# One load of two heads, or two loads of one head each: splitting the key and value loads of a decode attention kernel

## The chip, the cores and the metric

The kernel runs on one core of one Trainium2 chip. The metric is the time of one execution on the device, in microseconds (us), as the median of several runs. The profile is of one further execution. TensorE is called PE here, VectorE DVE, ScalarE ACT, GpSimd POOL; SP is the engine that does nothing here but issue transfers. All large transfers come from SP's queue and are carried out by the core's 16 DMA engines.

## The reference

One decode step for two sequences: a layer norm, attention of 32 query heads over the last 4096 positions of 8 cached key and value heads, and a small gated branch whose result multiplies the attention's output.

```python
xn = _layernorm(x)                                    # x: [2, 1, 512]
# attention: Hq, Hkv, Sk, Dh = 32, 8, 32768, 128; W = 4096; rep = 4
q = (xn @ wq).reshape(B, Sq, Hq, Dh).transpose(0, 2, 1, 3)
k = jnp.repeat(k_cache[:, :, Sk - W:, :], rep, axis=1)
v = jnp.repeat(v_cache[:, :, Sk - W:, :], rep, axis=1)
p = _softmax(jnp.einsum("bhqd,bhkd->bhqk", q, k) * Dh ** -0.5)
s = jnp.einsum("bhqk,bhkd->bhqd", p, v) ... @ wo      # wo: [4096, 512]
# gated branch: gelu, layer norm over half of it, two small products
g = _silu(_B_ref(xn, w_in, w_sp, b_sp, w_out))
return x + s * g
```

Everything is float32. Of each head 4096 rows of 512 bytes are read, 2 MiB, for the keys and again for the values. With 2 sequences and 8 heads that is 64 MiB of keys and values; the four weight matrices add 21.25 MiB.

## The kernel before, in words

**Units.** The 16 pairs of sequence and head are taken two heads at a time: 8 units (`NU`), each with a load of keys (`k`) and a load of values (`v`) of 4 MiB. A load fills one slot, a tile of 128 partitions with 32 KB each (`SLOT` = 8192 elements, 64 rows of the cache). Even partitions hold the unit's first head, odd ones its second: partition 2i has rows 64i to 64i+63 of the first head, partition 2i+1 the same rows of the second. The two heads lie 16 MiB apart in the cache, so the source of a load is written by hand as 64 steps of 32 KB, times 2 heads, times 8192 elements.

**The ring.** All large loads share four slots (pool `ring`). In the order in which SP issues them: `win`, `wout`, two halves of `wq`, then keys and values in the order k0, k1, v0, k2, v1, k3, v2, and so on to k7, v6, v7, and at last the output weights `wo` in pieces of 2, 2, 2, 1, 0.5, 0.25 and 0.25 MiB. A load waits until the slot's earlier content is used up: for keys, the last of four transposes on DVE (`turn`, tile `kt`), for values, the last of 16 products on PE (`values`, tile `acc`). After each load of keys or values but the first, SP also issues a small transfer from x into `rows`, of 2, 3, ... 15 and last 1 rows of 128 bytes (`load_rows`). No engine reads `rows`.

**Counters.** A transfer tells that it has landed by a counter (semaphore). Eight of them (`DMAHW0` to `DMAHW7`) are handed to the transfers in turn, in the order of the program. A transfer is issued only when the transfer that had the same counter before it, eight transfers back, has landed.

**A unit's work.** DVE turns the keys by four transposes (`kt<-k`), PE multiplies them with the queries (`sh`), ACT copies the result (`shs`), PE adds the shares into the unit's scores (`s`), DVE and ACT make the softmax of the unit before (`m`, `mg`, `mx`, `nb`, `p`, `pT`), and PE multiplies with the values (`acc`). The order on every engine is the order in which the program is written. The last unit is followed by the product with `wo` (`part`, `so`), the multiplication with the gate (`res`), and the store.

Names in the rows below carry a buffer's number, which differs between the two programs: keys of unit 3 are `k_296` before and `k_301` after, values of unit 3 `v_305` before and `v_313` after.

Of the kernel before, what the change touches and what calls it, by code (L numbers as in the profile page):

```python
# [14 lines left out]
P = 128  # L15
HQ, DH = 32, 128
# [26 lines left out]
def kernel(  # L43
# [14 lines left out]
    pe, dve, act, sp = (InOrder(tc, e) for e in (nc.tensor, nc.vector, nc.scalar, nc.sync))  # L58
    B, _, D = x.shape
    _, HKV, SK, _ = k_cache.shape  # L60
    W = min(4096, max(256, SK // 4))
# [8 lines left out]
    J = 2 * W // P  # L70
    JC = 512 // 32
    NCH = J // JC
    SLOT = J * DH
# [7 lines left out]
    def slot(name):  # L81
        return ring.tile([P, SLOT], F32, tag="slot", name=name)
# [18 lines left out]
    for a in range(2):  # L101
        t = slot(f"wq{a}")
# [11 lines left out]
    def load_unit(cache, u, name):  # L114

        b, w = divmod(u, NU // B)
        t = slot(f"{name}{u}")
        first = cache[b, 2 * w, SK - W :, :]
        src = bass.AP(tensor=first.tensor, offset=first.offset, ap=[[SLOT, P // 2], [SK * DH, 2], [1, SLOT]])
        sp.dma_start(t, src)  # L120
        return t.rearrange("p (j d) -> p j d", d=DH)


# [297 lines left out]
    for n in range(NU + 1):  # L421
        if n < NU:
            units[n].k = load_unit(k_cache, n, "k")
            if n > 0:
                load_rows(2 * n)
        if n > 0:
            units[n - 1].v = load_unit(v_cache, n - 1, "v")
            if n < NU:
                load_rows(2 * n + 1)
            else:  # L430
                load_rows(1)
# [4 lines left out]
    j = 0  # L436
    for i, piece in enumerate(pieces):
        t = slot(f"wo{i}").rearrange("p (j d) -> p j d", d=D)
        at = 0
        for n in piece:  # L440
            sp.dma_start(t[:, at : at + n, :], wo_v[:, j : j + n, :])
            blocks += [(t, at + a) for a in range(n)]
            at, j = at + n, j + n
# [49 lines left out]
    for n in range(EARLY):  # L493
        t, a = blocks[n]
# [5 lines left out]
    for n in range(EARLY, 32):  # L500
        if n == LATE:
            spread_quarters(so, parts, start=False, stop=False)
        t, a = blocks[n]
# [37 lines left out]
```

## Time and profile before

| | |
|---|---|
| time, median of 3 runs | 218.21 us (217.74 to 218.59) |
| span of the profiled execution, first to last instruction | 216.4 us |
| busy, PE / DVE / ACT | 154.9 / 108.6 / 44.0 us |
| moved by DMA | 89.55 MB, mean 414 GB/s over the span |
| chain that ended last, by engine | DMA 62%, DVE 19%, PE 16% |
| loads of keys, and of values | 8 and 8, 4096 KB each |

The profiled execution's own time is its span of 216.4 us and what lies around it; the median of the runs is 1.8 us longer than that span. The chain that ended last is found by going back from the last instruction to what released it, and so on. Times in the timeline count from the span's start.

### The profile page before, as it was taken

Reading aid. Unit: us, or ns where it says so; the run is one execution under the profiler, and the core shown is the slowest. Engines: PE = TensorE matmul, PEld = TensorE weight load, DVE = VectorE, ACT = ScalarE, POOL = GpSimd, SP = SyncE. Lnnn points to the kernel's source line nnn. Section 1 sums busy time; section 2 is a strip of 40 time slices with the busy share of each in tenths; the row PEclk is TensorE's granted clock in tenths of the full one; section 3 lists DMA queues with packets and bytes.
Section 4 is the critical chain, followed back from the end, with each engine's and each line's share of the span. In section 5 each row is a group of like instructions: output and inputs, shape, how many; then the busy total and the mean of one; then the engine's idle time right before and its main releaser. Section 6 shows DMA issues by size and latency. Waiting matters only on the chain.

```text
span 216.4 us, 2244 instructions
## 1 busy us (share of the span) xinstructions
PE 154.9 (72%) x866; PEld 43.0 (20%) x866; DVE 108.6 (50%) x176; ACT 44.0 (20%) x109; POOL 2.6 (1%) x14
## 2 busy tenths in 40 slices
PE   0173176518959957994995699459959967997973
PEld 0121121101212211221221222222222212231311
DVE  3505312569778089238806941695479089331001
ACT  5003310002221331042121304120331241242001
POOL 4000000000000000000000000000000000000000
PEclk9998569955997995899799589956996997999698
DMA  7999999999999999999999999999999999999990
GB/s 255 424 436 442 430 432 427 442 430 424 448 418 448 409 448 418 436 424 436 426 433 430 424 442 421 442 424 436 424 430 430 415 454 418 448 394 430 412 365 23
DMA packets 4169, 89.55 MB, mean 414 GB/s; under 512 B 686, under 2 KB 702, under 8 KB 1088
## 3 DMA queue, kind: packets, MB, share of 16 engines
q1 hardware_dynamic: 4152, 89.42, 96.8%
q8 instruction: 7, 0.11, 0.2%
q14 instruction: 2, 0.02, 0.0%
q10 hardware_dynamic: 8, 0.00, 0.0%
HBM read 89.41 MB, written 0.00 MB: 413 GB/s over the span
## 4 chain that ended last, share of the span: by engine, by line
DMA 62%; DVE 19%; PE 16%; issue 1%; DVEq 0%; SPq 0%
DMA k<-in_A_k_cache_dram 49%; DVE kt L37 16%; DMA wo<-in_A_wo_dram 8%; DMA win<-in_B_w_in_dram 5%; PE sh L37 5%; PE s L37 4%; PE z L37 3%; PE acc L37 2%; PE mo L37 1%; DVE pT L37 1%; PE so L37 1%; DVE m L37 1%; PE oT L37 0%; DVE mg L37 0%; DVE mx L37 0%
## 5 line engine op out<-in xcount | busy, mean ns | idle before, releaser
L37 DVE STREAM_TRANSPOSE kt<-k 128x2048 f32<-128x2048 f32 x32 | 72.7, 2295 | 41.6 <-DMA k<-in_A_k_cache_dram 41.6
L37 PE MATMUL sh<-kt,qbd 128*32 128x512 f32 x256 | 41.0, 704 | 17.8 <-DVE kt L37 17.7
L37 ACT ACTIVATE shs<-sh 128x512 f32<-128x512 f32 x32 | 19.1, 597 | 119.1 <-PE sh L37 119.1
L37 PE MATMUL s<-shs,add_dq 128*128 128x512 f32 x64 | 40.5, 739 | 0.0
L37 PE MATMUL acc<-v,pT 128*32 128x512 f32 x256 | 33.0, 657 | 0.2 <-DVE pT L37 0.2
L37 PEld LDWEIGHTS s<-shs,add_dq 128*128 128x128 f32 x64 | 11.0, 215 | 29.7 <-issue 25.4
L37 PEld LDWEIGHTS sh<-kt,qbd 128*32 128x32 f32 x256 | 6.5, 115 | 38.4 <-issue 23.9
L37 PEld LDWEIGHTS acc<-v,pT 128*32 128x32 f32 x256 | 7.8, 121 | 26.6 <-issue 19.0
L37 PE MATMUL mo<-l,same_r 128*128 128x2 f32 x16 | 3.5, 287 | 10.6 <-ACT p L37 10.6
L37 ACT ACTIVATE o<-acc,wd 128x128 f32<-128x128 f32 x32 | 9.1, 372 | 3.4 <-PE acc L37 3.4
L37 PE MATMUL part<-wo,oT 128*32 128x512 f32 x56 | 8.2, 720 | 1.8 <-DMA wo<-in_A_wo_dram 1.5
L37 ACT ACTIVATE p<-s,nb 128x256 f32<-128x256 f32 x16 | 7.6, 488 | 7.2 <-DVE nb L37 6.9
L37 PE MATMUL z<-win,xnT 128*32 128x448 f32 x32 | 5.6, 873 | 4.8 <-DMA win<-in_B_w_in_dram 4.8
L37 PE MATMUL q_ps<-wq,xnT 128*32 128x512 f32 x64 | 7.3, 594 | 1.9 <-DMA wq<-in_A_wq_dram 1.9
L37 PE MATMUL col<-o,sel 128*32 128x512 f32 x16 | 8.3, 601 | 0.4 <-ACT o L37 0.4
L37 DVE TENSOR_REDUCE m<-s 128x2 f32<-128x512 f32 x8 | 5.4, 670 | 5.4 <-PE s L37 5.4
L37 PE MATMUL y<-wout,hT 128*32 128x512 f32 x14 | 3.4, 1020 | 3.8 <-issue 3.8
L37 DVE TENSOR_TENSOR res<-so,gate 128x128 f32<-128x128 f32 x1 | 0.3, 290 | 11.7 <-PE so L37 11.7
L37 DVE STREAM_TRANSPOSE pT<-p 128x512 f32<-128x512 f32 x8 | 5.4, 674 | 1.2 <-ACT p L37 1.2
L37 ACT ACT_TABLE_LOAD x4 | 5.1, 1283 | 1.9 <-issue 1.9
L37 PE MATMUL xnT_ps<-ident,xn 2*128 2x2 f32 x4 | 0.6, 252 | 6.7 <-DVE xn L37 6.7
L37 PEld LDWEIGHTS mo<-l,same_r 128*128 128x128 f32 x16 | 2.8, 218 | 12.2 <-ACT p L37 12.2
(106 smaller groups left out, 63.1 us busy)
## 6 DMA issues: line engine op xcount, KB each, us to landing
k<-in_A_k_cache_dram SPq DMA_DIRECT2D x8, 4096.0 KB, 26.8
v<-in_A_v_cache_dram SPq DMA_DIRECT2D x8, 4096.0 KB, 25.2
wq<-in_A_wq_dram SPq DMA_DIRECT2D x2, 4096.0 KB
wo<-in_A_wo_dram SPq DMA_DIRECT2D x3, 2048.0 KB
win<-in_B_w_in_dram SPq DMA_DIRECT2D x1, 3584.0 KB
wout<-in_B_w_out_dram SPq DMA_DIRECT2D x1, 1792.0 KB, 15.1
wo<-in_A_wo_dram SPq DMA_DIRECT2D x1, 1024.0 KB
wo<-in_A_wo_dram SPq DMA_DIRECT2D x1, 512.0 KB
```

The lines of the kernel that those rows point to most:

```text
L37: return self.tc.keep_in_program_order(call(*args, **kwargs))
```

## The change

Each load of 4 MiB becomes two loads of 2 MiB, one per head. The first writes the even partitions of the slot, the second the odd ones, both from 64 steps of 32 KB that lie one behind the other in the cache. The bytes, their places in the slot, and everything that reads them stay as they are.

```diff
         b, w = divmod(u, NU // B)
         t = slot(f"{name}{u}")
-        first = cache[b, 2 * w, SK - W :, :]
-        src = bass.AP(tensor=first.tensor, offset=first.offset, ap=[[SLOT, P // 2], [SK * DH, 2], [1, SLOT]])
-        sp.dma_start(t, src)
+        for a in range(2):
+            sp.dma_start(t[a::2, :], cache[b, 2 * w + a, SK - W :, :].rearrange("(i j) d -> i (j d)", j=J))
         return t.rearrange("p (j d) -> p j d", d=DH)
```

SP's instructions, before, from the keys of unit 3 (`k_296`) to the values of unit 3 (`v_305`), with the counters and engines that each waits for:

```order
L37 DMA k_296<-in_A_k_cache_dram 128x1x8192 [waits DMAHW0_49,DVE_49]
L37 DMA rows<-in_A_x_dram 6x32 [waits DMAHW1_49]
L37 DMA v_299<-in_A_v_cache_dram 128x1x8192 [waits DMAHW2_49,PE_49]
L37 DMA rows<-in_A_x_dram 7x32 [waits DMAHW3_49]
L37 DMA k_302<-in_A_k_cache_dram 128x1x8192 [waits DMAHW4_49,DVE_49]
L37 DMA rows<-in_A_x_dram 8x32 [waits DMAHW5_49]
L37 DMA v_305<-in_A_v_cache_dram 128x1x8192 [waits DMAHW6_49,PE_49]
```

Eight transfers are four loads here, so the counter that a load waits for belongs to the load whose slot it fills. The same stretch after (`k_301` to `v_313`):

```order
L37 DMA k_301<-in_A_k_cache_dram 64x8192 [waits DMAHW5_49,DVE_49]
L37 DMA k_301<-in_A_k_cache_dram 64x8192 [waits DMAHW6_49]
L37 DMA rows<-in_A_x_dram 6x32 [waits DMAHW7_49]
L37 DMA v_305<-in_A_v_cache_dram 64x8192 [waits DMAHW0_49,PE_49]
L37 DMA v_305<-in_A_v_cache_dram 64x8192 [waits DMAHW1_49]
L37 DMA rows<-in_A_x_dram 7x32 [waits DMAHW2_49]
L37 DMA k_309<-in_A_k_cache_dram 64x8192 [waits DMAHW3_49,DVE_49]
L37 DMA k_309<-in_A_k_cache_dram 64x8192 [waits DMAHW4_49]
L37 DMA rows<-in_A_x_dram 8x32 [waits DMAHW5_49]
L37 DMA v_313<-in_A_v_cache_dram 64x8192 [waits DMAHW6_49,PE_49]
L37 DMA v_313<-in_A_v_cache_dram 64x8192 [waits DMAHW7_49]
L37 DMA rows<-in_A_x_dram 9x32 [waits DMAHW0_49]
```

A load and its `rows` are three transfers now, so eight transfers back is the load three before (its second half, for a first half) or the load two before (its first half, for `rows`). The values of unit 3 wait for `DMAHW6`, which the second half of the keys of unit 3 had.

On DVE, the first transpose of unit 3's keys (`kt_0_556`) and its neighbours before:

```order
L37 STREAM_TRANSPOSE kt_2_529<-k_290 128x2048
L37 STREAM_TRANSPOSE kt_3_539<-k_290 128x2048
L37 STREAM_TRANSPOSE kt_0_556<-k_296 128x2048 [waits DMAHW0_49,PE_49]
L37 TENSOR_REDUCE m_2_565<-s_503 128x2 [waits PE_49]
L37 TENSOR_TENSOR mg_567<-m_2_565,spot 128x32 [waits DVE_49]
```

The same place after (`kt_0_572`):

```order
L37 STREAM_TRANSPOSE kt_2_545<-k_293 128x2048
L37 STREAM_TRANSPOSE kt_3_555<-k_293 128x2048
L37 STREAM_TRANSPOSE kt_0_572<-k_301 128x2048 [waits DMAHW6_49,DMAHW5_49,PE_49]
L37 TENSOR_REDUCE m_2_581<-s_519 128x2 [waits PE_49]
L37 TENSOR_TENSOR mg_583<-m_2_581,spot 128x32 [waits DVE_49]
```

The order is the same; the transpose waits for two counters, one of each half. At the end of SP's program, from the values of unit 7 (`v_326`) to `wo`'s smaller pieces, before:

```order
L37 DMA v_326<-in_A_v_cache_dram 128x1x8192 [waits DMAHW4_49,DVE_49]
L37 DMA rows<-in_A_x_dram 1x32 [waits DMAHW5_49]
L37 DMA wo_329<-in_A_wo_dram 128x4096 [waits DMAHW6_49,PE_49]
L37 DMA wo_329<-in_A_wo_dram 128x4096 [waits DMAHW7_49]
L37 DMA x_91<-in_A_x_dram 8x1x128 [waits DMAHW0_49,Pool_49]
L37 DMA wo_333<-in_A_wo_dram 128x4096 [waits DMAHW1_49,DVE_49]
L37 DMA wo_335<-in_A_wo_dram 128x2048 [waits DMAHW2_49,PE_49]
```

And after (`v_341` is unit 7's values):

```order
L37 DMA v_341<-in_A_v_cache_dram 64x8192 [waits DMAHW3_49,DVE_49]
L37 DMA v_341<-in_A_v_cache_dram 64x8192 [waits DMAHW4_49]
L37 DMA rows<-in_A_x_dram 1x32 [waits DMAHW5_49]
L37 DMA wo_345<-in_A_wo_dram 128x4096 [waits DMAHW6_49,PE_49]
L37 DMA wo_345<-in_A_wo_dram 128x4096 [waits DMAHW7_49]
L37 DMA x_91<-in_A_x_dram 8x1x128 [waits DMAHW0_49,Pool_49]
L37 DMA wo_349<-in_A_wo_dram 128x4096 [waits DMAHW1_49,DVE_49]
L37 DMA wo_351<-in_A_wo_dram 128x2048 [waits DMAHW2_49,PE_49]
```

The counters of `wo`'s pieces are the same by number, but they were last held by other transfers: the first piece now waits for the keys of unit 7 (second half) to have landed, `x` for the first half of unit 6's values, and the third piece for the second half of these.

## The prediction

> **What bounds the kernel now.** I read the page first: its slices and the shares of the chain that ended last.
>
> ```profile
> DMA  7999999999999999999999999999999999999990
> ...
> DMA 62%; DVE 19%; PE 16%; issue 1%; DVEq 0%; SPq 0%
> ```
>
> The DMA engines are busy in every slice from the second to the last but one, and the chain hangs on them most. Then I asked for the stretches between landings of keys (engine columns, granted clock, DMA share, GB/s):
>
> ```profile
> 20.00:95.50 75.50, 52.59 (x286) 13.90 (x286) 41.10 (x66) 14.96 (x34) 0.00 (x0) 0.80 1.00 432
> 95.50:134.40 38.90, 31.19 (x159) 8.12 (x158) 22.50 (x26) 9.30 (x26) 0.00 (x0) 0.87 1.00 430
> 134.40:173.30 38.90, 31.24 (x162) 8.91 (x161) 23.39 (x28) 7.95 (x21) 0.00 (x0) 0.82 1.00 431
> 173.30:211.30 38.00, 31.69 (x186) 8.73 (x185) 14.72 (x24) 7.70 (x25) 0.00 (x0) 0.91 0.97 413
> ```
>
> The DMA share is 1.00 from 20 to 173 us, at 430 to 432 GB/s, while DVE is busy for little more than half of each stretch (41.10 of 75.50, 22.50 of 38.90). Next the chain in order of time; its DMA pieces run from a load's issue to its landing (start, length):
>
> ```profile
> 0.73 11.25 DMA win<-in_B_w_in_dram
> ...
> 17.76 29.17 DMA k<-in_A_k_cache_dram
> ...
> 69.78 25.73 DMA k<-in_A_k_cache_dram
> ...
> 107.61 26.79 DMA k<-in_A_k_cache_dram
> ...
> 149.18 24.15 DMA k<-in_A_k_cache_dram
> ...
> 193.27 17.98 DMA wo<-in_A_wo_dram
> 211.25 0.04 issue
> ```
>
> By their place in SP's order these are k0, k3, k5 and k7: loads 1, 6, 10 and 14 of the sixteen. They land at 17.76 + 29.17 = 46.93, at 95.51, at 134.40 and at 173.33. Thirteen loads lie between first and last: 126.40 / 13 = 9.72 us each, and the three parts agree (9.72, 9.72, 9.73). Four MiB in 9.72 us are 431 GB/s. So the loads land on a grid of 9.72 us: load n at 46.93 + 9.72 (n - 1). The grid gives 192.8 for the last load (v7); 7.5 MiB of `wo`, down to its 0.5 MiB piece, add 18.2 us at that rate, 211.0, and the last landing on the chain is at 211.25. 216.4 - 211.25 = 5.1 us of tail follow. The kernel is one row of transfers with hardly a gap, plus a tail. A microsecond added to the row is a microsecond at the end; a microsecond saved elsewhere is nothing.
>
> Last, the waits: what SP waits for (total, times, longest),
>
> ```profile
> SPq L37 <- DVE kt L37: 97.6, 8, 14.7
> ```
>
> and what DVE waits for with its first transpose of each unit's keys:
>
> ```profile
> DVE kt L37 <- DMA k<-in_A_k_cache_dram: 41.6, 8, 7.5
> ```
>
> DVE waits for keys in every unit, so the consumers are early, and SP stands idle for 97.6 us until DVE frees a slot.
>
> **The change, part by part.**
>
> *The issues.* Sixteen loads become 32, so SP issues 16 more. The timeline of SP's queue has the price:
>
> ```profile
> 88.17 0.54 SPq L37 DMA_DIRECT2D k<-in_A_k_cache_dram  x1
> 88.76 0.48 SPq L37 DMA_DIRECT2D rows<-in_A_x_dram  x1
> 91.32 0.54 SPq L37 DMA_DIRECT2D v<-in_A_v_cache_dram  x1
> ...
> 107.61 0.54 SPq L37 DMA_DIRECT2D k<-in_A_k_cache_dram  x1
> ...
> 169.64 0.84 SPq L37 DMA_DIRECT2D wo<-in_A_wo_dram  x2
> 173.40 0.64 SPq L37 DMA_DIRECT2D x<-in_A_x_dram  x1
> 185.44 9.20 SPq L37 DMA_DIRECT2D wo<-in_A_wo_dram  x5
> ```
>
> 16 x 0.54 = 8.6 us of SP, beside the row of transfers. The cover is what is still queued when a load is issued: k5 goes out at 107.61, when k4 (load 8, due at 114.97) and v3 (load 9, due at 124.69) are on the way, 17 us of work. An issue that comes 0.54 us later behind 17 us costs nothing; without that cover it would cost all of it. On path: 0.
>
> *The counters.* A first half now waits for the second half of the load three before, and `rows`, which stands ahead of the next load in SP's queue, for the first half of the load two before. For a load L this asks that load L-3 has landed, where before it was only its slot's old content, load L-4, that had to be used up. Where that bites: v3 (load 9) was issued at 91.32 and now waits for k3 (load 6), landed at 95.51, 4.2 us later; queued behind `rows` and v3 on SP is k5, which isn't due before 107.61. When v3 goes out at 95.51 the engines still have v2 and k4, 19.4 us of work. k5 waits for load 7, due at 46.93 + 58.32 = 105.25, before its slot is free at 107.61: no delay. In general the new wait ends when two whole loads are still on the way, so it can't drain the row. At the end, `wo`'s first piece goes from 169.64 to 173.33 (k7 landed), with v6 and v7 on the way, 19.4 us; `x`, behind it in the queue, to 46.93 + 9.72 x 13.5 = 178.2 (half of v6), needed only for the last addition at 213.39; `wo`'s third piece waits for v6 at 183.05, before its slot's 185.44; the pieces after it for the halves of v7, 187.9 and 192.8, and they are issued within 9.20 us of 185.44, up to 194.6. Sum of the waits on path: 0, and the cover is 17 us or more.
>
> *The waits of the readers.* DVE's first transpose of a unit waits for both halves, since it takes all 128 partitions; PE's products with the values too. The second half lands when the whole load did. The first half lands 4.86 us earlier and nobody may use it: gain 0.
>
> *The ends of transfers.* What is left is what one more transfer costs the engines between its neighbours. The trace of before has no load to 64 partitions; the nearest rows are `wo`'s small pieces, each of which PE waits for and starts on as it lands:
>
> ```profile
> 207.58 1.92 PE L37 MATMUL part<-wo,oT 128*32 128x512 f32 x16 [0.90 <-DMA wo<-in_A_wo_dram]
> 210.07 1.06 PE L37 MATMUL part<-wo,oT 128*32 128x512 f32 x8 [0.57 <-DMA wo<-in_A_wo_dram]
> 211.29 0.65 PE L37 MATMUL so<-wo,oT 128*32 128x128 f32 x16 [0.16 <-DMA wo<-in_A_wo_dram]
> ```
>
> The 1 MiB piece follows the 2 MiB piece by 210.07 - 207.58 = 2.49 us, the 0.5 MiB piece follows it by 1.22 us. At the loads' 9.72 us for 4 MiB the bytes alone take 2.43 and 1.215 us. So a transfer more costs between 0.005 and 0.06 us. I take 0.03, the middle, as both rows are equally near: 16 x 0.03 = 0.5 us, bounds 0.1 and 1.0. A gain is excluded: the rows of 32 KB stay as they are, and no transfer goes away.
>
> [...]
>
> *Sum.* 216.4 + 0.5 = 216.9 us of span. The runs' median is 1.8 us over the span, so 218.2 + 0.5 = **218.7 us**. With bounds of 0.1 to 1.0, and runs that spread by 0.4 either way, this case's own range is 217.9 to 219.6.
>
> A measurement of this kernel can tell about 0.5% from no change, 1.1 us: faster is below 217.1, slower above 219.3.
>
> **The rivals.**
>
> *A half moves at half the rate.* This is the rival on the other side, and its place is the row of transfers from 46.93 - 9.72 on. Each transfer now writes 64 partitions, every other one, and every large row of the trace is a load to 128. [...] Nothing would hide it, as the DMA share is 1.00: it decides from the first per cent lost on. [...] Chance 0.15.
>
> [...] No trace here shows a load to 64 partitions.
>
> *A gap at each half.* [...] The nearest row, far off, is SP's 0.54 us for an issue: 16 x 0.54 = 8.6 us, 226.8, and at half of it 222.5. Against it: `wo`'s pieces follow each other with 0.06 us at most, and they were queued the same way. For it: SP waits for counters between issues now, and that was not so for the pieces. It decides where a half is issued later than its forerunner ends, which the 17 us of cover speak against. Chance 0.16.
>
> *Faster.* The row of transfers has some slack: 89.55 MB at 431 GB/s are 207.8 us, and it runs from 0.73 to 211.25, 210.5 us. If loads issued in smaller portions kept the engines closer together, up to 2.7 us could go: 215.5. Against it: the share of 1.00 in the middle, with the slack at the start and the end, which the change doesn't touch. Chance 0.05.
>
> **How the numbers follow.** The forecast has 0.64, half rate 0.15, a gap 0.16, faster 0.05. The likeliest gives 218.7. The range starts at 217.4, a little under the forecast's own for a small gain, and reaches to 226.8, the gap's bound: it leaves out half rate and most of the faster case, hardly 0.2. Faster by over 0.5%: 0.05. Slower: half rate and gap, 0.31. The same: 0.64.
>
> **What would show it.** Right, if the new profile has k0, k3, k5 and k7 still 9.7 to 9.8 us apart per load, the DMA share at 1.00 with 429 GB/s or more, 32 issues of 2048 KB, v3's first half issued at about 95.5 instead of 91.3 with no gap behind it, and the same tail of 5 us. The counters are the wrong step if slices with a DMA share under 9 tenths turn up where SP waits for a transfer. The ends of transfers are mis-sized if the share stays at 1.00 or just under and a load takes over 9.8 us. Half rate would show in GB/s near 216 in all stretches to 173 us at a share that stays full, with DVE's waits for keys many times the 41.6 us.

## The result, and the profile after

| | before | after |
|---|---|---|
| time, median of 5 runs | 218.03 us (217.74 to 218.59) | 219.05 us (218.64 to 219.28) |
| span of the profiled execution | 216.4 us | 217.5 us |

The ratio is 1.0038, with a 95% interval of 1.0020 to 1.0056: slower by 0.4 to 1.2 us. The median is 1.0 us over before, and 0.35 us over the forecast of 218.7. The ratios in this document are of each kernel's faster executions alone; only two kernels further down, the blocks and the eighths, have executions over 1.5% slower than their fastest.

The page of the changed kernel has nineteen instructions more than before's 2244, and one of the two queues that fetch instructions (`q14`) moved four packets instead of two:

```profile
span 217.5 us, 2263 instructions
...
DMA  7999999999999999999999999999999999999970
...
q14 instruction: 4, 0.03, 0.0%
```

The DMA engines are as full as before in every slice but the last but one (7 instead of 9), which ends at 212.1 us here and at 211.0 before. In the chain of waits the same four loads of keys stand as before (start, length):

```profile
17.79 28.91 DMA k<-in_A_k_cache_dram
69.53 25.76 DMA k<-in_A_k_cache_dram
107.94 26.20 DMA k<-in_A_k_cache_dram
149.61 23.43 DMA k<-in_A_k_cache_dram
...
213.18 0.30 DVE res L37
```

They land at 46.70, 95.29, 134.14 and 173.04: 126.34 / 13 = 9.72 us per load, the grid of before to the hundredth. The first product with the gate (`res`) starts at 213.18; the chain of before has

```profile
213.07 0.30 DVE res L37
```

So of the 1.1 us between the two spans 1.0 us arises after the start of `res`, where only the output's store is left. What SP waits for, before,

```profile
SPq L536 <- DMA out_dram<-res: 0.8, 1, 0.8
```

and after:

```profile
SPq L37 <- DMA v<-in_A_v_cache_dram: 57.5, 14, 4.6
SPq L37 <- DMA k<-in_A_k_cache_dram: 47.6, 14, 4.6
SPq L37 <- DVE kt L37: 21.0, 7, 5.2
...
SPq L535 <- DMA out_dram<-res: 1.9, 1, 1.9
```

The counters' new waits are there: SP now stands idle for landings (57.5 and 47.6 us) where it stood idle for DVE (97.6 before, 21.0 now), and nothing hangs on that. The one wait that matters is the last: SP waits 1.9 instead of 0.8 us for the store of 4 KB, which lands 2.8 us after the start of its issue instead of 1.7. The view of DMA queues for the last microseconds of the changed kernel, 213 to 217, says what else was moved then:

```profile
q14 instruction: 1, 0.01, 0.5%
q1 hardware_dynamic: 12, 0.00, 0.4%
```

In before, the same view from 213 to the end has no instruction packet:

```profile
q1 hardware_dynamic: 12, 0.00, 0.5%
```

The packet of 8 KB begins 1.44 us after the store's issue at 213.82, at 215.26, and takes 0.31 us. Six of the store's eight rows of 512 bytes start by 215.15; the last two start at 215.57 and 215.59, as the packet ends. The store tells of its landing in four parts: three come at 215.50 to 215.53, the last at 216.61. In before all eight rows start within 0.1 us, and the last part comes at 215.43.

### The profile page after: what moved, and what is told of

It is laid out like the page before. It is cut to its first block, busy times and chain, and to the rows that moved or that the text cites. A ratio compares the mean times of both kernels' runs of the same rounds, so it can differ in the third digit from the quotient of the medians.

```text
span 217.5 us, 2263 instructions
## 1 busy us (share of the span) xinstructions
PE 152.2 (70%) x866; PEld 43.0 (20%) x866; DVE 108.6 (50%) x176; ACT 44.0 (20%) x109; POOL 2.6 (1%) x14
## 4 chain that ended last, share of the span: by engine, by line
DMA 63%; DVE 21%; PE 11%; issue 1%; SPq 1%; ACT 0%; DVEq 0%; ACTq 0%
DMA k<-in_A_k_cache_dram 48%; DVE kt L37 17%; DMA wo<-in_A_wo_dram 10%; DMA win<-in_B_w_in_dram 5%; PE sh L37 3%; PE z L37 2%; PE part L37 2%; PE s L37 2%; DVE pT L37 1%; SPq L37 1%; PE mo L37 1%; DVE m L37 1%; PE oT L37 1%; DVE wd L37 0%; DVE ls L37 0%
## 5 line engine op out<-in xcount | busy, mean ns | idle before, releaser
L37 PE MATMUL sh<-kt,qbd 128*32 128x512 f32 x256 | 41.7, 716 | 18.2 <-DVE kt L37 18.2
L37 PE MATMUL s<-shs,add_dq 128*128 128x512 f32 x64 | 39.6, 726 | 0.0
L37 PE MATMUL acc<-v,pT 128*32 128x512 f32 x256 | 31.7, 636 | 0.2 <-DVE pT L37 0.2
L37 PE MATMUL z<-win,xnT 128*32 128x448 f32 x32 | 4.9, 769 | 5.0 <-DMA win<-in_B_w_in_dram 5.0
```

Source lines behind the costliest of these rows:

```text
L37: return self.tc.keep_in_program_order(call(*args, **kwargs))
```

## The experiments

Theory A is the prediction's: each transfer more costs the row of transfers 0.03 to 0.06 us. Two others came from the traces: a fetch of instructions beside the output store, because SP's program is longer (B) or because DVE's is (C). (The counts of DVE's and SP's instructions that are given here, 194 and 80 before, include two each that the traces don't show.) For C, the double waits of DVE's first transposes count: two of them need a wait instruction more, which makes 196 instructions on DVE instead of 194. With 16 issues on SP and one wait on PE that is the nineteen.

**Both kernels once more.** No edit.

> The kernel before, once more, for a second trace and as a measure of the scatter. Both theories: 218.0 us within 0.4, ratio 1.000 within 0.002, keys 9.72 us per load apart, output store landed 1.7 us after its issue as in the first trace.

> The changed kernel, once more, for a second trace. Both theories: ratio 1.002 to 1.006. Theory A (each transfer more costs the row of transfers some 0.03 to 0.06 us): the last piece of the output weights lands 0.5 to 1 us later than before. Theory B (the row of transfers is as fast as before; SP's program is 16 instructions longer, so that a fetch of instructions of 8 KB falls beside the output store and holds one of its four engines up): the last piece lands within 0.3 us of before, and the store takes about 1 us longer from issue to landing, with a count of four instruction packets in the smaller instruction queue instead of two.

Measured: before 0.9993 (0.9984 to 1.0003), the changed kernel 1.0039 (1.0023 to 1.0054). In the second traces the store waits 0.8 and 1.6 us, `res` starts at 212.74 and 213.23, and the packet comes 1.16 us after the start of the store's issue in the changed kernel. In before it comes only at 216.72, after the last instruction. Over all eleven traces of this study with rows of 32 KB at full rate, `res` starts at 212.71 to 213.47, on average at 212.96 with whole loads and at 213.14 with split ones: 0.2 us within a scatter of 0.8. What differs between the kernels is the store. In all fourteen traces of this study the two go together: five have a packet 1.15 to 1.44 us behind the start of the store's issue, and there SP waits 1.5 to 1.9 us; nine have none between the start of its issue and its landing, and there SP waits 0.7 to 0.8 us.

**A longer program on SP.**

```diff
         sp.dma_start(t, src)
+        nc.sync.drain()
```

> Loads of both heads in one, as before, with one empty instruction (a drain of SP) after each, so that SP's program has the 96 instructions of the changed kernel. Theory A: no more transfers than before, ratio 1.000 within 0.002. Theory B: the time of the changed kernel, ratio 1.003 to 1.005, 0.6 to 1.1 us over before, all of it behind the issue of the output store.

Measured: 1.0014 (0.9999 to 1.0030), 218.31 us. The store waits as in before:

```profile
SPq L537 <- DMA out_dram<-res: 0.8, 1, 0.8
```

SP's 96 instructions bring a packet more, at 196.9 us, amid the loads of weights. The upper end of the interval touches B's 1.003, but B's longer wait at the store isn't there in the trace, which is of an execution of 217.93 us.

**Split, without the small transfers.**

```diff
     def load_rows(n):
-        sp.dma_start(rows[:n, n - 1, :], bass.AP(tensor=x.tensor, offset=x.offset, ap=[[32, n], [1, 32]]))
+        return
```

> Split loads as in the changed kernel, without the 15 small transfers that nobody reads (their part of the computation is nothing). SP has 45 transfers instead of 60, about as many instructions as before. Theory A: 32 loads still have 16 ends more, less what the 15 small ones cost (0 to 0.05 each): ratio 1.000 to 1.004. Theory B: the fetch is gone from the end, ratio 1.000 within 0.002, and the store lands 1.7 us after its issue.

Measured: 1.0038 (1.0024 to 1.0052). This speaks against B: SP has 15 instructions fewer than the changed kernel, and the store waits 1.5 us, the packet 1.16 us behind its issue. A alone would allow the ratio, but not where the time goes.

**Two instructions without work on DVE, loads as before.** A drain in the set-up, which takes a wait with it; the scheduler moves a few copies there, all before 12 us.

```diff
     dve.tensor_copy(sel[:, 24:32], rowr)
+    nc.vector.drain()
```

> Loads of both heads in one, as before, with two instructions without work on DVE in the set-up before 12 us, so that DVE's program has 196 instructions as the changed kernel's has, where before has 194. Theory A (32 ends of transfers): ratio 1.000 within 0.002, store landed 1.7 us after its issue. Theory B (SP's program is longer): the same, since SP has its 80 instructions. Theory C (the double waits make DVE's program two instructions longer, and its last fetch of 8 KB falls beside the output store): ratio 1.003 to 1.005, an instruction packet within 1.6 us of the store's issue, SP's wait for the store 1.5 to 1.9 us instead of 0.8.

Measured: 1.0053 (1.0032 to 1.0074), 219.12 us, with whole loads and SP's program as before. What SP waits for, and the queues from 213 to 217:

```profile
SPq L537 <- DMA out_dram<-res: 1.6, 1, 1.6
```

```profile
q14 instruction: 1, 0.01, 0.8%
q1 hardware_dynamic: 12, 0.00, 0.4%
```

The whole loss of the change, without the change.

**Two instructions fewer on DVE, loads split.**

```diff
-        dve.tensor_mul(spot[:, a], ap(grpm, 0, [[1, G], [0, NCH]]), ap(diag, 0, [[0, G], [1, NCH]]))
-        dve.tensor_scalar_mul(spot[:, a], spot[:, a], am[:, a : a + 1])
+        dve.scalar_tensor_tensor(
+            spot[:, a], ap(grpm, 0, [[1, G], [0, NCH]]), am[:, a : a + 1], ap(diag, 0, [[0, G], [1, NCH]]),
+            op0=ALU.mult, op1=ALU.mult,
+        )
```

> Split loads as in the changed kernel; on DVE two products of the set-up are joined with the two that scale them, so that DVE has 194 instructions as before. SP has its 96. Theory A: ratio 1.002 to 1.006 as for the changed kernel. Theory B: the same. Theory C: no instruction packet beside the store, SP's wait for it 0.8 us, ratio 1.000 within 0.002.

Measured: 0.9999 (0.9988 to 1.0011), 218.06 us. The page's first line and the store's wait:

```profile
span 216.8 us, 2261 instructions
```

```profile
SPq L537 <- DMA out_dram<-res: 0.8, 1, 0.8
```

Split loads, 96 instructions on SP, and the time of before: A and B are out. The fetch isn't gone: a packet of 8 KB comes at 217.45, 0.65 us after the last instruction, where nothing waits for it.

**Nine more on DVE, loads split.** Eight drains at the place of the one above.

> Split loads with nine more instructions without work on DVE in the set-up, 205 in all against 196. Theories A and B: as the changed kernel, ratio 1.002 to 1.006. [...] If the fetch is tied to the program's end instead of to a place in it, 1.004 stays.

Measured: 1.0005 (0.9995 to 1.0016), 218.16 us. The packet is there, but 35 us earlier than in the changed kernel; the store's wait, and the queues from 179 to 182:

```profile
SPq L543 <- DMA out_dram<-res: 0.8, 1, 0.8
```

```profile
q1 hardware_dynamic: 72, 1.34, 106.0%
q14 instruction: 1, 0.01, 0.7%
```

It starts at 180.11, amid the loads, and costs nothing that can be measured: 1.0005 is not the 1.002 to 1.006 of A and B, nor the 1.004 of a fetch tied to the program's end. So the fetch isn't tied to that end, and it is its time that matters. What sets that time stays open: at 180.11 DVE has started 180 of the 203 instructions in its trace, and in the changed kernel 191 of 194 when the packet comes, which is the same place neither from the start nor from the end.

**Quarters.** 64 loads of 1 MiB, of every fourth partition, without the small transfers; DVE has 204 instructions. The new lines:

```diff
+        for a in range(2):
+            for h in range(2):
+                first = cache[b, 2 * w + a, SK - W + h * J :, :]
+                src = bass.AP(tensor=first.tensor, offset=first.offset, ap=[[2 * SLOT, P // 4], [1, SLOT]])
+                sp.dma_start(t[a + 2 * h :: 4, :], src)
```

> Each load in four of 1 MiB (every fourth partition), 64 loads instead of 32, and without the small transfers that nobody reads. DVE has 204 instructions. Theory A: 48 ends more than before at 0.03 to 0.06 us: 1.4 to 2.9 us more, ratio 1.006 to 1.013, keys 9.8 to 9.9 us per load apart. Theory C: ends cost nothing measurable, keys 9.72 us per load apart, no fetch beside the store, ratio 1.000 within 0.003.

Measured: 0.9990 (0.9980 to 1.0000), 217.94 us. Against the whole loads without the small transfers,

> The kernel before without the 15 small transfers that nobody reads. Every theory: ratio 0.998 to 1.000; it shows whether the quarters' 0.999 comes from these.

measured 0.9997 (0.9985 to 1.0010), 48 more transfers cost 0.0007 less, with intervals of about 0.001 on both sides, each against before in a round of its own: at most some 0.2 us for 48, 0.004 us each. The last stretch of the chain through the keys ends at 154.07 + 19.40 = 173.47, 0.14 us after before's 173.33. Nothing of A's term is seen. That the quarters are faster than before isn't shown either: their interval reaches 1.0000.

**By columns.** All 128 partitions, in two halves of 16 KB each.

```diff
-        sp.dma_start(t, src)
+        for h in range(2):
+            ...
+                ap=[[SLOT, P // 2], [SK * DH, 2], [1, SLOT // 2]],
+            ...
+            sp.dma_start(t[:, h * (SLOT // 2) : (h + 1) * (SLOT // 2)], src)
```

> Each load in two of 2 MiB by columns: all 128 partitions, first the first 16 KB of each, then the second. 32 transfers, DVE 194 instructions, SP 96, PE 499 as in the changed kernel. Theory C: no packet beside the store, SP's wait for it 0.8 us; what is left is the cost of rows of 16 instead of 32 KB, which the trace must show, 0 to 2 us, ratio 1.000 to 1.009. If PE's 499th instruction were what matters, the store would wait 1.5 to 1.9 us.

Measured: 1.0050 (1.0034 to 1.0066), 219.28 us, and the store's wait is 0.8 us: PE's one instruction more, which this kernel has too, isn't the cause. The loss is in the rows. The stretches of the prediction's table have

```profile
20.00:95.50 75.50, 53.57 (x286) 15.15 (x286) 43.70 (x69) 15.07 (x35) 0.00 (x0) 0.80 1.00 428
95.50:134.40 38.90, 30.94 (x167) 9.22 (x166) 22.73 (x26) 9.22 (x26) 0.00 (x0) 0.91 1.01 428
134.40:173.30 38.90, 30.46 (x159) 9.50 (x154) 23.51 (x28) 8.03 (x22) 0.00 (x0) 0.82 1.00 426
```

4 GB/s less than before in the mean. A row of 32 KB takes 1213 ns at the shortest in before, a row of 16 KB 611 ns here: two of these are 9 ns more for the same bytes, and by the means, 1218 and 615.5 ns, 13 ns more. At 8 rows of 32 KB per load and DMA engine (9.72 us at 1218 ns a row) and 16 loads that is an estimate of 1.2 to 1.7 us, against 1.2 us measured. Here it is `res` that starts late, at 214.18.

**By blocks of 64 partitions.** Partitions 0 to 63, then 64 to 127, every byte where it was. The new lines:

```diff
+        for h in range(2):
+            first = cache[b, 2 * w, SK - W + h * (W // 2) :, :]
+            src = bass.AP(tensor=first.tensor, offset=first.offset, ap=[[SLOT, P // 4], [SK * DH, 2], [1, SLOT]])
+            sp.dma_start(t[64 * h : 64 * h + 64, :], src)
```

> Each load in two of 2 MiB by blocks of partitions: 0 to 63 and 64 to 127, each with both heads, so that every partition gets what it had before. DVE has 196 instructions as the changed kernel. [...]

Measured: 1.726 (1.718 to 1.734), 375 and 379 us. From 60 to 340 us of the traced execution, which took 382 us:

```profile
60.00:340.00 280.00, 139.58 (x596) 37.85 (x596) 88.11 (x103) 33.68 (x89) 0.00 (x0) 0.66 1.00 211
```

The DMA share is 1.00 and the rate 211 GB/s, half: the engines are all at work, each half as fast. Half of the rows of 32 KB take 2.54 us or more, against 1.22 in before. The rival of half rate is real, for these halves.

**Eighths.** As the quarters, with `range(4)`, steps of 4 in the source and of 8 in the partitions.

> Each load in eight of 0.5 MiB (every eighth partition), 128 loads, without the small transfers. Each piece waits by its counter for the same piece of the load before, so only one load of 9.72 us is on the way at any time; DVE has 220 instructions. If one load is cover enough and ends cost nothing: ratio 0.998 to 1.002. If ends cost 0.03 us each: 112 x 0.03 = 3.4 us, 1.015. If the counters drain the queue now, slices with a DMA share under 9 tenths and 1.02 or more.

Measured: 1.670 (1.664 to 1.676), 363 and 366 us, against all three cases of the expectation. The same stretch:

```profile
60.00:340.00 280.00, 138.90 (x596) 37.25 (x592) 88.47 (x105) 34.65 (x92) 0.00 (x0) 0.67 1.00 222
```

Half rate again, at a full share, and half of the rows of 32 KB take 2.35 us or more: not the counters, which would have left the engines idle, and not the ends, which would not lengthen a row. Sixteen partitions 8 apart (222 GB/s) are about as bad as 64 in a block (211 GB/s); 32 that are 4 apart run at full rate (the quarters, 429 to 433 GB/s in the three stretches from 20 to 173 us), and so do 64 that are 2 apart (the changed kernel, 429 to 433 GB/s in the same stretches). Why the rate halves in two of the four no trace shows. Whether the counters would drain the queue at this depth stays open, since half rate hides it.

## Why the prediction was right, and where it was wrong

**What bounds the kernel: right.** The loads stand on the same grid of 9.72 us, at a DMA share of 1.00 to 1.01 from 20 to 173 us, and what changed the time lay on the row of transfers (blocks, eighths, columns) or in the tail.

**The issues and the counters: right, shown.** SP's timeline after has the values of unit 3 where they were forecast (95.5; 91.32 before):

```profile
95.35 1.11 SPq L37 DMA_DIRECT2D v<-in_A_v_cache_dram  x2
```

SP's wait turned from DVE to landings, and no slice of the DMA engines fell below nine tenths while SP waited for loads, from 34 to 178 us.

**The ends of transfers: the term that failed.** It was all of the 0.5 us. The quarters bound it at some 0.004 us each, 0.1 us for the sixteen. The row it was read from, 2.49 us for a 1 MiB piece, held no price of an end: `wo`'s pieces are cut by columns, the 1 MiB piece has eight rows of 8 KB per DMA engine, and at 309 ns a row, the shortest in the trace, to 313 ns, the mean, these are 2.47 to 2.51 us. So the shorter rows account for the 0.06 us that were read as a transfer's end.

**The waits of the readers: wrong.** They were put at nothing, since both halves have landed when the whole would have. That is so, but two of the second waits are an instruction each (196 on DVE instead of 194). These two moved DVE's fetch beside the store: 0.7 to 1.1 us of wait, all of the measured 1.0. The total came out near the measurement by luck: a cost that isn't there stood in for one that was overlooked.

**The tail: wrong.** "The same tail of 5 us" was named as what would show the forecast right, and the tail is where the time went.

**The rivals.** Half rate was given 0.15, as the author's estimate; no trace shows how the rows of a transfer are divided among the engines. With every other partition in a half it did not come: 429 to 433 GB/s, against 430 to 432 before. Where the partitions are chosen otherwise it did: at twice 9.72 us for each of the 16 loads the forecast of 218.7 would be 155.5 us longer, an estimate of 374 us from the grid, and the blocks took 375 and 379 us, the eighths 363 and 366. A gap at each half and a faster row of transfers did not come either: the loads stay 9.72 us apart.

## What to carry to other kernels

When transfers queue behind each other, as here, cutting them in two or in four need cost nothing that can be measured (split loads 218.06 and quarters 217.94 us here, with 218.20 for before in the same round). Look instead at which partitions each piece writes (429 to 433 GB/s with every other or every fourth, 211 with blocks of 64, 222 with every eighth) and how long its rows are (426 to 428 GB/s with 16 KB, 430 to 432 with 32 KB). Count the instructions that an edit adds on every engine, waits included: two on DVE put a fetch of the program beside the store here, and a fetch that cost nothing in a full queue (180 us) cost 1 us beside a lone transfer at the end (215 us). A difference of 0.4% can lie wholly in the tail.

## What the runs showed of the hardware that was not expected

In the four traces at full rate, a fetch of 0.31 to 0.52 us holds two rows of the store up by 0.2 to 0.4 us, but the store's landing by 0.8 to 1.1 us: SP sees it 1.0 us after the last row in the changed kernel and 0.4 us in before. Where the rest comes from stays open, as does what sets the moment of DVE's fetch.

The packets at the end are of 8 KB. With one at 180 us the time was 218.16 us in all, with one at 215 us 219.05.
